# Batches 0 and 1 of a fused attention and feed-forward kernel: keys put into token order, v loaded in one DMA per block, weights issued at other places, four zero matmuls, attention steps placed by weight

## The chip, the cores and the metric

One core of a Trainium2 chip runs the whole program. The metric is the device time of one execution in microseconds (us). The engines are TensorE (PE; its weight loads are shown apart, as PEld), VectorE (DVE), ScalarE (ACT), GpSimd (POOL) and SyncE (SP). SP and POOL also issue DMAs.

## The reference, cut to what matters

Attention with a linear position bias (ALiBi) and a sliding window of 128 tokens, for 8 batches of 8 heads, 576 tokens and head size 64; then a feed-forward layer over all 8 x 576 = 4608 tokens. Inputs and output are fp32.

```python
scores = (q @ k.transpose(0, 1, 3, 2)) / 8.0
rel    = pos[:, None] - pos[None, :]
scores = where((rel >= 0) & (rel < 128), scores - slopes[h] * abs(rel), -1e9)
x      = softmax(scores) @ v                     # 8 batches, 8 heads
x      = x.transpose(0, 2, 1, 3).reshape(4608, 512)
h      = x @ w_in                                # 512 x 2048
out    = (h * sigmoid(beta * h)) @ w_out         # 2048 x 512
```

## The kernel before, in words

**Tokens, blocks, groups.** A batch has four full blocks of 128 tokens and a tail of 64. Attention works by batch and by pair of heads; the feed-forward layer works by groups of 512 tokens (g = 0 to 8), whose transposed input lies in the ring XT. The first half of the layer (`Hm`, L484) is, for each of 16 slices j of the 2048 features, four matmuls from W1 into a PSUM tile (hps, or hpx for some slices of group 0), a tanh on ACT (sig, L502) and the product on DVE (gT, L503). The second half (`OS`, L512) is 16 matmuls from gT and W2 for each 128 tokens, a copy on ACT (osb, L524) and a store. The weights arrive as four chunks each, issued by POOL (`load_w1` L268, `load_w2` L272); these DMAs cast from fp32 to bf16.

**Batches 0 and 1** have a path of their own. `get_pair` (L235) loads two heads of q or k, four neighbouring tokens to a partition; POOL casts to bf16 (`cast_pair`, L252); `TP` (L280) transposes both on PE into one PSUM tile and copies them to qkT, two copies on DVE. With c the place of a token in its group of four and r the number of the group, the copies put each block of 128 tokens in the order (c, r) instead of token order, for queries and keys alike. So v has to lie in the same order: `get` (L216) loads each full v block of these batches in four DMAs, one for each c (L222 to L228). `SP_` (L309) makes the scores of a pair of heads in two visits ("A" and "B"): matmuls that put the bias table into PSUM (SS), the query-key matmuls (L331), one exp on ACT to pt. `PVP` (L348) multiplies by v (L360) and normalizes on DVE (`norm`, L342: a reciprocal zs and a product xnp). `XP` (L367) transposes by a matmul with the permutation matrix perm, which puts queries back into token order, and DVE copies to XT (L372). The tails of both batches go through `TT`, `SCT`, `PV`, `X`. The constants for this path (ktok, qtok, rel, table, perm) come from `constants` (L109); qtok minus ktok is the distance of query and key in their permuted places. `constants_late` (L147) makes the table of the tails, relt and tablet.

**Batches 2 to 7** are loaded by block, cast on POOL, transposed by DMA (`DT`, L394). `SC` (L407) makes the scores of a pair; the exp (L430, four for a pair) takes its bias from the tile bias, one column for each head and half, and DVE multiplies by a mask (L434). `PV` (L445) and `X` (L465) follow.

**bias and the masks** are made in `constants_masks` (L189): POOL makes kpos by an iota (L193), 128x1, then the masks; sixteen small DVE instructions (L206) make bias from kpos.

**What sets the order.** PE, SP and POOL run in the order in which the program is written (L591). ACT and DVE have that too in the opening only (L592 to L645, batch 0 and the first slices of group 0); after it, a scheduler of the language chooses their order when the program is built. Every engine's queue is in order. After the opening, the program issues on SP the loads of batch 1 (the first waits for W1's second chunk, by `after(g, w1[1])`) and the tails of both batches; on POOL, in this order, the casts of batch 1 with W2's four chunks among them, then the casts of both tails, then `constants_masks`:

```python
        cast_pair(1, 2)
        w2 = [load_w2(0), load_w2(1)]
        cast_pair(1, 3)
        cast_v(1, 2)
        cast_v(1, 3)
        w2 += [load_w2(2), load_w2(3)]
        for b in range(2):
            cast_qk(b, 4)
            cast_v(b, 4)
        constants_masks()
```

On PE, the list `second` (L680) gives the steps of batch 1, two after each slice j of group 0's first half from j = 5 on. From group 1 on, `spread` (L717) places the attention steps of batches 2 to 7 (the list `att`: `SC`, `PV`, `X`, and the jobs that load, cast and transpose the next batch) between the matmul groups of the feed-forward layer: the same number of steps after each group.

**Buffers that matter here.** The loads share 13 tiles (fst). PE's transposes, PVP, XP, PV and X share two PSUM tiles (psum_t, tag "t"), hps has two, and all scores go through the one tile SS, except that visit "B" of batch 0 has a tile of its own, SX.

Of the kernel before, what the change touches and what calls it, by code (L numbers as in the profile page):

```python
# [15 lines left out]
P = 128  # L16
# [3 lines left out]
def kernel(  # L20
# [85 lines left out]

    def constants():  # L109
        nc.vector.memset(zeros[:], 0.0)  # L110
        nc.vector.memset(warm[:], 0.0)
        nc.scalar.activation(out=warm[:], in_=warm[:], func=ACTF.Exp)
        for _ in range(8):
            nc.tensor.matmul(
                SS[:, 0, :], lhsT=zeros[:, 0:P], rhs=zeros[:], start=True, stop=True,
                skip_group_check=True)
        for c in range(4):
            nc.gpsimd.iota(
                ktok[32 * c : 32 * c + 32], pattern=[[0, 1]], base=c, channel_multiplier=4,
                allow_small_or_imprecise_dtypes=True,  # L120
            )
        nc.gpsimd.iota(
            qtok[:].rearrange("p (c r) -> p c r", c=4), pattern=[[1, 4], [4, 32]], base=0, channel_multiplier=0,
            allow_small_or_imprecise_dtypes=True,
        )
        make_identity(nc, ident[:])
        nc.gpsimd.iota(
            nat[:], pattern=[[1, P]], base=0, channel_multiplier=0,
            allow_small_or_imprecise_dtypes=True,
        )  # L130
        nc.vector.tensor_scalar(
            out=qtok[:], in0=qtok[:], scalar1=ktok[:, 0:1], scalar2=None, op0=ALU.subtract)
        for a, cmp in ((0, ALU.is_lt), (1, ALU.is_ge)):
            nc.vector.tensor_scalar(
                out=pen[:], in0=qtok[:], scalar1=0.0, scalar2=FAR, op0=cmp, op1=ALU.mult)
            nc.vector.scalar_tensor_tensor(
                out=rel[:, a], in0=qtok[:], scalar=float(P * a), in1=pen[:], op0=ALU.add,
                op1=ALU.add)
        nc.vector.tensor_copy(out=rel[:, 2], in_=rel[:, 0])
        for h in range(H):  # L140
            nc.vector.tensor_scalar_mul(table[:, h], rel[:], -slopes[h] / qscale)
        for i in range(2):
            nc.vector.memset(VS[i][:, :, :, D : D + 1], 1.0)
        nc.vector.tensor_scalar(
            out=perm[:], in0=nat[:], scalar1=ktok[:, 0:1], scalar2=None, op0=ALU.is_equal)

    def constants_late():  # L147
        nc.gpsimd.iota(
            relt[:, 0], pattern=[[1, 64]], base=0, channel_multiplier=-1,
            allow_small_or_imprecise_dtypes=True,  # L150
        )
        nc.gpsimd.affine_select(
            out=relt[:, 0], in_=relt[:, 0], pattern=[[1, 64]], base=0, channel_multiplier=-1,
            compare_op=ALU.is_ge, fill=FAR,
        )
        for c in range(4):
            rows = slice(32 * c, 32 * c + 32)
            nc.gpsimd.iota(
                relt[rows, 1], pattern=[[1, 64]], base=P - c, channel_multiplier=-4,
                allow_small_or_imprecise_dtypes=True,  # L160
            )
            nc.gpsimd.affine_select(
                out=relt[rows, 1], in_=relt[rows, 1], pattern=[[-1, 64]], base=c - 1,
                channel_multiplier=4, compare_op=ALU.is_ge, fill=FAR,
            )
# [47 lines left out]
    fs = {}  # L213
    staged = {}

    def get(what, b, sb, eng=None):  # L216

        rows = ROWS[sb]
        src = {"q": q, "k": k, "v": v}[what]
        f = fst_pool.tile([P, H, D], F32, name="fst", tag="fst")  # L220
        fs[what, b, sb] = f
        if what == "v" and b < 2 and sb < 4:  # L222
            for c in range(4):
                (eng or nc.sync).dma_start(
                    out=f[32 * c : 32 * c + 32],
                    in_=src[b, :, P * sb : P * sb + P, :].rearrange(
                        "h (r c) d -> c r h d", c=4)[c],
                )  # L228
            return
        return nc.sync.dma_start(  # L230
            out=f[0:rows],
            in_=src[b, :, P * sb : P * sb + rows, :].rearrange("h p d -> p h d"),
        )
# [18 lines left out]
    def cast_pair(b, p):  # L252
        t = bst_pool.tile([P, 2, 4, 2 * D], BF16, name="bst", tag="bst")
        staged[b, "p", p] = t
        for i, w in enumerate("qk"):
            nc.gpsimd.tensor_copy(
                out=t[:, i].rearrange("r c (h d) -> r h c d", d=D),
                in_=fs.pop((w, b, "p", p))[:].rearrange("r h (c d) -> r h c d", d=D))
# [21 lines left out]
    def TP(b, p):  # L280
        src = staged.pop((b, "p", p))
        tps = psum_t.tile([P, 2, 4, P], BF16, name="tps", tag="t")
        for i in range(2):
            for c in range(4):
                nc.tensor.transpose(out=tps[:, i, c], in_=src[:, i, c], identity=ident[:])
        qk = QK[b % 2]
        for i in range(2):
            nc.vector.tensor_copy(
                out=qk[:, i, p, 0:FULL].rearrange("d (n c r) -> d c n r", n=4, c=4),
                in_=tps[:, i].rearrange("d c (n r) -> d c n r", n=4))  # L290

    def TT(b):

# [252 lines left out]
    def pvx(b, qbs):  # L546
        r = []
        for qb in qbs:
            r += [(None, lambda g=g, qb=qb: PV(b, qb, g)) for g in range(2)]
            if qb != qbs[0]:  # L550
                r.append(((b, qb - 1), lambda qb=qb: X(b, qb - 1)))
        r.append(((b, qbs[-1]), lambda: X(b, qbs[-1])))
        return r

    def merged(a, c):
# [11 lines left out]
    for b in range(2, B):  # L567
        here = []
        for m in range(2):
            a = [(None, lambda b=b, m=m, p=p: SC(b, m, p)) for p in range(NP)]  # L570
            here += merged(a, before)
            before = pvx(b, ((0, 1), (2, 3, 4))[m])
        if b + 1 < B:
            js, all_, n = jobs(b + 1), here, len(here)
            here = []
            for i, step in enumerate(all_):
                while js and js[0][0] * n <= 23 * i:
                    here.append((None, js.pop(0)[1]))
                here.append(step)
            here += [(None, j) for _, j in js]  # L580
        att += here
    att += before
    place = {key: n + 1 for n, (key, _) in enumerate(att) if key}

    def place_of(tok):
        b, s = divmod(tok - 1, S)
# [4 lines left out]
    with tc.manual_schedule(engines={ENG.PE, ENG.SP, ENG.Pool}):  # L591
        with tc.manual_schedule(engines={ENG.Activation, ENG.DVE}):  # L592
            for w in ("p0", "p1", "v0", "v1", "p2", "p3", "v2", "v3"):
                n = int(w[1])
                if w[0] == "p":
                    get_pair("q", 0, n)
                    get_pair("k", 0, n)
# [30 lines left out]
            PVP(0, "B", 0)  # L628
            PVP(0, "B", 1)
            XP(0, 0)  # L630
            PVP(0, "B", 2)
            XP(0, 1)
            PVP(0, "A", 3)
            XP(0, 2)
            PVP(0, "B", 3)
            betas()
            constants_late()
            opening.close()
# [13 lines left out]
        g = get_pair("q", 1, 0)  # L652
        after(g, w1[1])
        get_pair("k", 1, 0)
        for n in range(1, NP):
            get_pair("q", 1, n)
            get_pair("k", 1, n)
            if n == 1:
                get("v", 1, 0)
                get("v", 1, 1)  # L660
# [68 lines left out]

        def wrap(it, n):  # L730
# [55 lines left out]
```

## Time and profile before

| | |
|---|---|
| median of 3 runs | 364.48 us (363.73 to 366.2) |
| the profiled execution | 362.3 us |
| its span in the trace | 360.4 us |
| mean granted PE clock | 0.981 |
| data read and written | 36.71 MB and 9.44 MB |
| DMA packets under 512 B | 125840 of 136511 |

The profile shows one execution. Its span runs from the first to the last instruction; the time of an execution is a little longer. Busy time is given in us and as a share of the span for each engine; the clock is a share of full speed and is given by slice of the span. The DMA share is the mean busy time of the core's 16 DMA engines as the records tell it; in this trace it passes 1 in places. In the lists of instructions, `out<-in` names the tiles, `L` the line in the kernel, and the words in brackets say how long the engine had waited before and for what. The page's lines on where the chain of work that ended last spent its time:

```profile
PE 70%; DMA 11%; DVE 8%; ACT 5%; issue 3%; SPq 2%; POOL 1%; POOLq 0%; ACTq 0%
PE ops L518 32%; PE hps L495 28%; DMA fst<-in_k_dram 5%; PE SS L420 4%; ACT pt L430 3%; DMA fst<-in_v_dram 3%; DVE pt L434 3%; DVE gT L503 3%; PE pv L459 2%; PE pv L455 2%; PE xt L470 2%; DMA W<-in_moe_w_in_dram 2%; ACT sig L502 1%; DMA fst<-in_q_dram 1%; SPq L240 1%
```

The first line adds up the chain by engine, the second by engine, tile and line. Six tenths of the chain are the matmuls of the feed-forward layer.

### The profile page before, as it was taken

The numbers are of one execution on the slowest core, as the hardware profiler recorded it, in microseconds if no ns is written. First come the engines' busy times: TensorE is split into PE (matmuls) and PEld (weight loads), VectorE is DVE, ScalarE is ACT, GpSimd is POOL, SyncE is SP. The second block draws the span as 40 slices with busy tenths as digits, with TensorE's granted clock in tenths as the row PEclk, the third lists the DMA queues.
The fourth block names the chain that finished last, engine by engine and source line by source line (L and its number), as shares of the span: only waits on it lengthen the run. The fifth ranks groups of instructions, "written<-read, shape, count | busy, mean of one in ns | idle before, by whom it ended". The sixth has DMA issues, their size and how long they took to land.

```text
span 360.4 us, 6325 instructions
## 1 busy us (share of the span) xinstructions
PE 327.8 (91%) x2323; PEld 155.4 (43%) x2365; DVE 202.6 (56%) x448; ACT 206.4 (57%) x392; POOL 109.6 (30%) x214
## 2 busy tenths in 40 slices
PE   6777847798799999989999999999999999999995
PEld 2343413343345444444444444444444444544442
DVE  6456528554565578456738764875487546615500
ACT  2615623456756679457746776676677755525511
POOL 5597445403543442333132414131200010010010
PEclk9989969999899999999999999999999999999999
DMA  6799899995999999992928792962100010020012
GB/s 172 181 198 249 172 185 206 207 159 125 200 201 244 249 188 222 210 218 62 214 88 178 163 218 93 189 156 65 60 0 32 31 58 29 3 84 4 31 58 87
DMA packets 136511, 49.45 MB, mean 137 GB/s; under 512 B 125840, under 2 KB 134048, under 8 KB 136480
## 3 DMA queue, kind: packets, MB, share of 16 engines
q1 hardware_dynamic: 129536, 35.94, 51.4%
q0 software_dynamic: 6944, 13.11, 14.3%
q8 instruction: 18, 0.29, 0.4%
q14 instruction: 13, 0.11, 0.1%
HBM read 36.71 MB, written 9.44 MB: 128 GB/s over the span
## 4 chain that ended last, share of the span: by engine, by line
PE 70%; DMA 11%; DVE 8%; ACT 5%; issue 3%; SPq 2%; POOL 1%; POOLq 0%; ACTq 0%
PE ops L518 32%; PE hps L495 28%; DMA fst<-in_k_dram 5%; PE SS L420 4%; ACT pt L430 3%; DMA fst<-in_v_dram 3%; DVE pt L434 3%; DVE gT L503 3%; PE pv L459 2%; PE pv L455 2%; PE xt L470 2%; DMA W<-in_moe_w_in_dram 2%; ACT sig L502 1%; DMA fst<-in_q_dram 1%; SPq L240 1%
## 5 line engine op out<-in xcount | busy, mean ns | idle before, releaser
L495 PE MATMUL hps<-XT,W 128*128 128x512 bf16 x543 | 141.9, 385 | 5.4 <-DVE gT L503 2.6
L502 ACT ACTIVATE sig<-hps,beta_h 128x512 bf16<-128x512 f32 x140 | 96.0, 691 | 79.4 <-PE hps L495 73.9
L518 PE MATMUL ops<-W,gT 128*128 128x512 bf16 x552 | 137.9, 380 | 1.6 <-issue 0.5
L503 DVE SCALAR_TENSOR_TENSOR gT<-sig,hps 128x512 bf16<-128x512 bf16 x140 | 94.9, 683 | 62.8 <-ACT sig L502 62.2
L430 ACT ACTIVATE pt<-SS,bias 128x256 bf16<-128x256 f32 (+1 forms) x192 | 75.0, 477 | 13.0 <-PE SS L420 13.0
L495 PEld LDWEIGHTS <-W 128*128 128x128 bf16 x576 | 52.2, 98 | 61.6 <-issue 11.9
L518 PEld LDWEIGHTS <-gT 128*128 128x128 bf16 x576 | 52.3, 98 | 57.1 <-issue 1.9
L531 POOL DMA_DIRECT2D out_dram<-osb x34 | 18.4, 542 | 188.7 <-ACT osb L524 188.7
L434 DVE TENSOR_TENSOR pt<-pt,mask 128x1024 bf16<-128x1024 bf16 x48 | 38.1, 795 | 16.4 <-ACT pt L430 16.1
L524 ACT ACTIVATE osb<-ops 128x512 f32<-128x512 f32 x36 | 21.7, 603 | 41.3 <-PE ops L518 40.9
L262 POOL CAST vs<-fst 128x512 bf16<-128x512 f32 (+1 forms) x40 | 24.1, 613 | 25.8 <-DMA fst<-in_v_dram 24.4
L344 DVE RECIPROCAL zs<-pv 128x4 f32<-128x4 f32 (+1 forms) x80 | 13.7, 175 | 28.6 <-PE pv L459 19.2
L345 DVE TENSOR_TENSOR xn<-pv,zs 128x256 bf16<-128x256 f32 (+1 forms) x64 | 26.8, 421 | 1.6
L249 POOL CAST bst<-fst 128x512 bf16<-128x512 f32 (+1 forms) x32 | 20.2, 630 | 11.2 <-DMA fst<-in_q_dram 8.7
L420 PE MATMUL SS<-qkT 64*128 64x256 bf16 (+2 forms) x240 | 19.2, 254 | 2.8 <-ACT pt L430 2.8
L459 PE MATMUL pv<-vs,pt 128*128 128x65 bf16 x240 | 20.6, 193 | 0.5 <-DVE pt L434 0.5
L476 DVE COPY XT<-xt 128x512 bf16<-128x512 bf16 (+1 forms) x32 | 12.3, 384 | 15.3 <-PE xt L470 15.0
L250 POOL CAST bst<-fst 128x512 bf16<-128x512 f32 (+1 forms) x32 | 19.6, 613 | 3.7 <-DMA fst<-in_k_dram 3.3
L459 PEld LDWEIGHTS <-pt 128*128 128x128 bf16 x240 | 16.0, 97 | 7.1 <-DVE pt L434 0.6
L337 ACT ACTIVATE pt<-SS 128x768 bf16<-128x768 f32 (+1 forms) x12 | 10.6, 881 | 14.5 <-PE SS L331 14.5
L420 PEld LDWEIGHTS <-qkT 64*128 64x128 bf16 x240 | 8.2, 94 | 22.4 <-issue 22.0
L455 PE MATMUL pv<-vs,pt 128*128 128x65 bf16 x192 | 17.4, 193 | 0.1
(77 smaller groups left out, 172.2 us busy)
## 6 DMA issues: line engine op xcount, KB each, us to landing
out_dram<-osb POOLq DMA_DIRECT2D x34, 256.0 KB, 2.5
fst<-in_q_dram SPq DMA_DIRECT2D x32, 256.0 KB, 4.8
fst<-in_k_dram SPq DMA_DIRECT2D x32, 256.0 KB, 4.9
fst<-in_v_dram SPq DMA_DIRECT2D x24, 256.0 KB, 3.9
fst<-in_v_dram SPq DMA_DIRECT2D x32, 64.0 KB, 4.1
W<-in_moe_w_in_dram POOLq DMA_DIRECT2D x4, 512.0 KB, 6.7
W<-in_moe_w_out_dram POOLq DMA_DIRECT2D x4, 512.0 KB, 9.1
fst<-in_q_dram SPq DMA_DIRECT2D x8, 128.0 KB, 3.7
```

What stands on the lines that cost most here:

```text
L262: return nc.gpsimd.tensor_copy(out=VS[b % 2][0:rows, sb, :, 0:D], in_=fs.pop(("v", b, sb))[0:rows])
L345: nc.vector.tensor_tensor(out=xn, in0=pv[0:nq, :, 0:D], in1=zs[0:nq].broadcast_to([nq, 4, D]), op=ALU.mult)
L420: nc.tensor.matmul(o, lhsT=qk[64 * e : 64 * e + 64, 1, p, P * kb : P * kb + P], rhs=qk[64 * e : 64 * e + 64, 0, p, P * kb : P * kb + nq], ...
L430: nc.scalar.activation(out=pt[:, e, cols], in_=sps[:, e, cols], func=ACTF.Exp, scale=qscale, bias=bias[:, half, h : h + 1],)
L434: nc.vector.tensor_tensor(out=pt[:], in0=pt[:], in1=masks[m][:], op=ALU.mult)
L455: nc.tensor.matmul(pv[:, hl, 0 : D + 1], lhsT=weights(b, qb - 1, h, 1), rhs=vs[:, qb - 1, h, 0 : D + 1], start=True, stop=False,)
L459: nc.tensor.matmul(pv[:, hl, 0 : D + 1], lhsT=weights(b, qb, h, 0), rhs=vs[:, qb, h, 0 : D + 1], start=qb == 0, stop=True,)
L495: nc.tensor.matmul(hps[:], lhsT=W1[:, c, bass.ts(j, P)], rhs=XT[:, c, c0 : c0 + TOKG], start=(c == 0), stop=(c == NDM - 1),)
L502: nc.scalar.activation(out=sig[:], in_=hps[:], func=ACTF.Tanh, scale=beta_h[:, j : j + 1])
L503: nc.vector.scalar_tensor_tensor(out=gts[g][:, j, :], in0=sig[:], scalar=1.0, in1=hps[:], op0=ALU.add, op1=ALU.mult)
L518: nc.tensor.matmul(ops_, lhsT=gT[:, j, i * P : i * P + P], rhs=W2[:, j, :], start=(j == 0), stop=(j == NFF - 1),)
L524: nc.scalar.mul(osb[:], ops_, 0.5)
```

## The change

- **Keys in token order.** In `TP` the copy of k moves from DVE to ACT and writes the keys in token order (a strided output); the copy of q stays on DVE and keeps the order (c, r). k is loaded, cast and transposed before q.
- **v in one DMA.** With keys in token order, `get` loads every v block of batches 0 and 1 like all others, in one DMA instead of four.
- **Constants.** qtok becomes the distance by itself (an iota that also counts down over partitions), so a DVE subtraction goes; the second half of relt takes one iota and one select instead of four of each.
- **XT copies of batch 0** go from DVE to ACT.
- **Zero matmuls.** `idle(1)`, one 512-column matmul of zeros into SS, stands on PE ahead of `XP(0, 0)`, `XP(0, 1)` and `XP(0, 2)` and behind `PVP(0, "B", 3)`.
- **Weights.** W1's first chunk is issued before `cast_pair(0, 3)` and its second right behind it; the second was behind `cast_v(0, 3)`. W2's last two chunks are issued before `cast_v(1, 2)` and `cast_v(1, 3)` instead of behind them.
- **Steps by weight.** A step of `att` has a weight: 3 for `SC`, 2 for `PV` and `X`, 0 for a job; `spread` gives each matmul group the same weight of steps, not the same number.

```diff
+    def idle(n):
+        for _ in range(n):
+            nc.tensor.matmul(
+                SS[:, 0, :], lhsT=zeros[:, 0:P], rhs=zeros[:], start=True, stop=True,
+                skip_group_check=True)
...
         nc.gpsimd.iota(
-            qtok[:].rearrange("p (c r) -> p c r", c=4), pattern=[[1, 4], [4, 32]], base=0, channel_multiplier=0,
-            allow_small_or_imprecise_dtypes=True,
+            qtok[:].rearrange("p (c r) -> p c r", c=4), pattern=[[1, 4], [4, 32]], base=0,
+            channel_multiplier=-1, allow_small_or_imprecise_dtypes=True,
         )
...
-        nc.vector.tensor_scalar(
-            out=qtok[:], in0=qtok[:], scalar1=ktok[:, 0:1], scalar2=None, op0=ALU.subtract)
...
-        if what == "v" and b < 2 and sb < 4:
-            for c in range(4):
-                (eng or nc.sync).dma_start(
-                    out=f[32 * c : 32 * c + 32],
-                    in_=src[b, :, P * sb : P * sb + P, :].rearrange(
-                        "h (r c) d -> c r h d", c=4)[c],
-                )
-            return
...
-        for i, w in enumerate("qk"):
+        for i, w in ((1, "k"), (0, "q")):
             nc.gpsimd.tensor_copy(
...
-        for i in range(2):
+        for i in (1, 0):
             for c in range(4):
                 nc.tensor.transpose(out=tps[:, i, c], in_=src[:, i, c], identity=ident[:])
         qk = QK[b % 2]
-        for i in range(2):
-            nc.vector.tensor_copy(
-                out=qk[:, i, p, 0:FULL].rearrange("d (n c r) -> d c n r", n=4, c=4),
-                in_=tps[:, i].rearrange("d c (n r) -> d c n r", n=4))
+        nc.scalar.copy(
+            out=qk[:, 1, p, 0:FULL].rearrange("d (r c) -> d c r", c=4), in_=tps[:, 1])
+        nc.vector.tensor_copy(
+            out=qk[:, 0, p, 0:FULL].rearrange("d (n c r) -> d c n r", n=4, c=4),
+            in_=tps[:, 0].rearrange("d c (n r) -> d c n r", n=4))
...
-        nc.vector.tensor_copy(
+        (nc.vector.tensor_copy if b else nc.scalar.copy)(
             out=XT[:, p, b * S : b * S + FULL], in_=xt[:].rearrange("d n q -> d (n q)"))
...
+            w1.append(load_w1(0))
             cast_pair(0, 3)
-            w1.append(load_w1(0))
+            w1.append(load_w1(1))
             TP(0, 3)
...
             cast_v(0, 2)
             cast_v(0, 3)
-            w1 += [load_w1(n) for n in range(1, 4)]
+            w1 += [load_w1(n) for n in range(2, 4)]
             PVP(0, "B", 0)
             PVP(0, "B", 1)
+            idle(1)
             XP(0, 0)
...
         cast_pair(1, 3)
+        w2 += [load_w2(2), load_w2(3)]
         cast_v(1, 2)
         cast_v(1, 3)
-        w2 += [load_w2(2), load_w2(3)]
...
-            start = done
+            total, at = sum(w for _, _, w in att[done:target]), 0
             for n, it in enumerate(items):
                 it()
                 if waiting:
                     store()
-                to = start + (target - start) * max(0, n + 1 - first) // (last - first)
-                while done < min(target, to):
+                to = total * max(0, n + 1 - first) / (last - first)
+                while done < target and at + att[done][2] / 2 <= to:
                     att[done][1]()
+                    at += att[done][2]
                     done += 1
```

`constants_masks` and its place in the program are not touched by the diff.

More of the change, by code (lines that the diff above doesn't have):

```diff
@@ L112, in constants @@
         nc.scalar.activation(out=warm[:], in_=warm[:], func=ACTF.Exp)
[L113 to L116, printed above, removed]
+        idle(8)
         for c in range(4):
@@ L155, in constants_late @@
         )
-        for c in range(4):
[L157 to L160, printed above, removed]
-            )
[L162 to L165, printed above, removed]
+        nc.gpsimd.iota(
+            relt[:, 1], pattern=[[1, 64]], base=P, channel_multiplier=-1,
+            allow_small_or_imprecise_dtypes=True,
+        )
+        nc.gpsimd.affine_select(
+            out=relt[:, 1], in_=relt[:, 1], pattern=[[-1, 64]], base=-1,
+            channel_multiplier=1, compare_op=ALU.is_ge, fill=FAR,
+        )
         for h in range(H):
@@ L214, with get @@
     staged = {}
-    def get(what, b, sb, eng=None):
+    def get(what, b, sb):
         rows = ROWS[sb]
@@ L221, in get @@
         fs[what, b, sb] = f
-        if what == "v" and b < 2 and sb < 4:
-            for c in range(4):
-                (eng or nc.sync).dma_start(
-                    out=f[32 * c : 32 * c + 32],
-                    in_=src[b, :, P * sb : P * sb + P, :].rearrange(
-                        "h (r c) d -> c r h d", c=4)[c],
-                )
-            return
         return nc.sync.dma_start(
@@ L548, in pvx @@
         for qb in qbs:
-            r += [(None, lambda g=g, qb=qb: PV(b, qb, g)) for g in range(2)]
+            r += [(None, lambda g=g, qb=qb: PV(b, qb, g), 2) for g in range(2)]
             if qb != qbs[0]:
-                r.append(((b, qb - 1), lambda qb=qb: X(b, qb - 1)))
-        r.append(((b, qbs[-1]), lambda: X(b, qbs[-1])))
+                r.append(((b, qb - 1), lambda qb=qb: X(b, qb - 1), 2))
+        r.append(((b, qbs[-1]), lambda: X(b, qbs[-1]), 2))
         return r
@@ L569 @@
         for m in range(2):
-            a = [(None, lambda b=b, m=m, p=p: SC(b, m, p)) for p in range(NP)]
+            a = [(None, lambda b=b, m=m, p=p: SC(b, m, p), 3) for p in range(NP)]
             here += merged(a, before)
@@ L577 @@
                 while js and js[0][0] * n <= 23 * i:
-                    here.append((None, js.pop(0)[1]))
+                    here.append((None, js.pop(0)[1], 0))
                 here.append(step)
-            here += [(None, j) for _, j in js]
+            here += [(None, j, 0) for _, j in js]
         att += here
     att += before
-    place = {key: n + 1 for n, (key, _) in enumerate(att) if key}
+    place = {key: n + 1 for n, (key, _, _) in enumerate(att) if key}
     def place_of(tok):
@@ L595 @@
                 if w[0] == "p":
+                    get_pair("k", 0, n)
                     get_pair("q", 0, n)
-                    get_pair("k", 0, n)
                 else:
@@ L626 @@
             cast_v(0, 3)
-            w1 += [load_w1(n) for n in range(1, 4)]
+            w1 += [load_w1(n) for n in range(2, 4)]
             PVP(0, "B", 0)
             PVP(0, "B", 1)
+            idle(1)
             XP(0, 0)
             PVP(0, "B", 2)
+            idle(1)
             XP(0, 1)
             PVP(0, "A", 3)
+            idle(1)
             XP(0, 2)
             PVP(0, "B", 3)
+            idle(1)
             betas()
@@ L650, in tail @@
                     lambda: X(b, 4)]
-        g = get_pair("q", 1, 0)
+        g = get_pair("k", 1, 0)
         after(g, w1[1])
-        get_pair("k", 1, 0)
+        get_pair("q", 1, 0)
         for n in range(1, NP):
+            get_pair("k", 1, n)
             get_pair("q", 1, n)
-            get_pair("k", 1, n)
             if n == 1:
```

## Prediction

> **What bounds the kernel now.** I read the engine shares first, then the chain of waits in order of time, then the timeline where the chain leaves the PE, the busy time by stretch, and the DMA records.
>
> ```profile
> PE 327.8 (91%) x2323; PEld 155.4 (43%) x2365; DVE 202.6 (56%) x448; ACT 206.4 (57%) x392; POOL 109.6 (30%) x214
> PEclk9989969999899999999999999999999999999999
> ```
>
> The PE is busy 91% of the span and from 100 us on has hardly a gap; its 33 us of idle time lie in the first 100 us and at the very end. This change works on the first 100 us. The chain there:
>
> ```profile
> 41.09 8.25 DMA fst<-in_v_dram
> ...
> 50.06 0.32 PE pv L360 x3
> ...
> 59.36 0.97 DVE bias L206 x16
> ```
>
> A v load of batch 1 holds the PE until 50.06, and at 59.36 sixteen small DVE instructions (bias, made from kpos) are on the path. The timeline at those places:
>
> ```profile
> 41.64 0.34 PE L360 MATMUL pv<-vs,pt 128*128 128x65 bf16 x6
> ...
> 42.37 0.34 PE L331 MATMUL SS<-qkT 64*128 64x256 bf16 x4
> ...
> 50.06 0.32 PE L360 MATMUL pv<-vs,pt 128*128 128x65 bf16 x3 [4.92 <-POOL vs L262]
> ...
> 58.24 0.61 POOL L262 CAST vs<-fst 64x512 bf16<-64x512 f32 x1 [3.73 <-DMA fst<-in_v_dram]
> ...
> 58.81 0.14 POOL L193 IOTA kpos<- 128x1 f32 x1
> ...
> 59.27 1.05 DVE L206 TENSOR_SCALAR bias<-kpos 128x1 f32<-128x1 f32 x16
> ```
>
> Read the last three together: POOL makes kpos only after the cast of batch 1's last v block, and that cast waited 3.73 us for its load. So kpos at 58.81 is a time of the DMA stream, not of POOL. Busy time by stretch (PE, PEld, DVE, ACT, POOL, granted clock, DMA share, GB/s):
>
> ```profile
> 15.50:18.00 2.50, 1.92 (x22) 0.84 (x20) 0.99 (x4) 1.55 (x2) 1.97 (x4) 1.00 0.48 38
> 18.00:36.00 18.00, 14.00 (x119) 7.24 (x119) 10.67 (x26) 6.57 (x10) 14.73 (x35) 0.91 1.15 223
> 36.00:38.00 2.00, 0.88 (x12) 0.30 (x6) 0.85 (x2) 1.02 (x1) 0.00 (x0) 1.00 0.43 107
> ...
> 41.00:42.50 1.50, 1.50 (x16) 0.75 (x14) 1.16 (x5) 1.50 (x2) 1.50 (x4) 1.00 0.62 93
> ...
> 50.00:54.00 4.00, 3.72 (x22) 1.68 (x22) 1.61 (x5) 1.48 (x2) 3.84 (x8) 0.50 1.17 154
> ...
> 88.00:92.00 4.00, 1.65 (x13) 0.78 (x13) 1.98 (x3) 3.52 (x10) 0.00 (x0) 0.97 1.26 229
> 92.00:95.00 3.00, 2.67 (x10) 0.78 (x10) 0.88 (x2) 2.17 (x6) 1.45 (x3) 0.50 1.35 222
> ```
>
> The DMA engines are full (share about 1.15) from 10 to 62 us but for three holes. After each PE pause the clock is 0.50 for some microseconds. Records between 46 and 48 us, where v loads and the W2 loads are both under way (number, MB, share):
>
> ```profile
> q0 software_dynamic: 311, 0.32, 92.8%
> q1 hardware_dynamic: 312, 0.08, 29.6%
> ```
>
> The two queues alternate one record for one record, whatever the record's size: a 1024-byte weight record goes with every 256-byte record of v.
>
> **The step that decides.** Outside the opening DVE's order is the scheduler's, and the built order of the changed kernel moves bias. DVE's queue there, in order (changed kernel's lines):
>
> ```
> gT  <- sig,hps        (j = 6)
> qkT <- tps            (q of batch 1, pair 1)
> bias <- kpos   x16    waits for POOL
> zs, xnp <- pv         (PVP(1,"A",0))
> gT  <- sig,hpx        (j = 7)
> qkT <- tps            (q of batch 1, pair 2)
> ```
>
> Before, bias stands 25 instructions later, behind the norm of the second-last PVP of batch 1, where DVE arrives at 59.27, just after kpos. POOL's order is written out by hand and still has kpos behind all casts of batch 1 and of both tails. DVE runs its queue in order (the trace of before shows it in the built order), so from about 36 us, where it finishes the q copy of pair 1 (36.43 + 0.42 before), it now waits for kpos. Queued behind the wait: the norm of PVP(1,"A",0). PE goes on until PVP(1,"A",1), whose PSUM slot that norm must free (41.64 before).
>
> When is kpos? Before: 58.81. Holes that the one-DMA v loads and the earlier W1 can fill, at a full share of 1.15: 2.50 x (1 - 0.48/1.15) = 1.5, 2.00 x (1 - 0.43/1.15) = 1.3, 1.50 x (1 - 0.62/1.15) = 0.7, together -3.4. Against this, all of W2 is now issued before batch 1's last two v casts and so alternates ahead of the tail loads; before, 230 weight records ran between 58 and 61 us, after the v load: 230 x 0.096 us / 16 engines = +1.4. Between W1's second chunk and its last two, which wait for the cast of v, a new hole of 0 to 1.4 us, estimated from chunk 0 (5.5 us from issue to landing, 512 x 0.1 / 16 = 3.2 of it records): +0.7. So kpos at 58.81 - 3.4 + 1.4 + 0.7 = 57.5; bounds 55.4 (holes filled, nothing given back) and 60.9 (no hole filled, both costs).
>
> Then 0.15 of iota, 1.05 of bias, 0.6 of zs and xnp (0.17 + 0.42): PVP(1,"A",1) at 59.3. gT 0.69 and the q copy 0.42 more: the scores of SP_(1,"A",2) at 60.55 instead of 42.37: **+18.2**.
>
> The Trainium skill ("DMA: Bandwidth & Descriptors", Rules for kernel authors) advises to issue a DMA early and wait late, since the fixed setup then overlaps; by that rule the earlier W2 costs nothing and the sum is 1.4 lower. The row above disagrees: beside W2 that v load took 8.25 us, the ones just before it 2.7 to 3.3.
>
> **The other parts.**
> - The stall of 4.92 at 50.06 goes: PVP(1,"B",0) comes at about 63, long after its v (49.34 before, at most a few us later). **-4.9.** Late next is nothing of DMA: both tails and W2 have landed too.
> - bias leaves its old place, where 0.97 of it was on the path before the XT copy at 60.24: **-1.0**.
> - Clock: PE idles some 20 us and restarts at 0.50. Before, the same happened at 50.06 and cost 3.72/2 = 1.9 until 54. Taken as the same, **0**; bounds 0 and +1.9 (twice that). The Trainium skill ("TensorE: Matmul & The Clock Gate", Part 1) has free-running windows of 3.4 us, so 3.4 to 6.8 us cold; by it the loss is 1.7 to 3.4 and the sum -0.2 to +1.5.
> - Steps by weight: between 88 and 95 PE loses 2.35 idle and 2.67/2 = 1.3 at half clock, because score steps of batch 2 stand close and ACT paces them. In the new order no two stand without a matmul group (0.86) between, but ACT's work is the same: **-1.5**; bounds -4 (all gone) and +1.5 (later steps crowded instead).
> - All else lies under DVE's wait, 17 us of cover, and counts 0. If the cover were gone: four zero matmuls 4 x 0.22 to 0.42, at most 1.7; eight k copies on ACT, each priced between 0.60 (osb, 597 ns for 512 columns) and 0.81 (exp, 768 columns), nearest 0.60, and as built the q copy (0.42) waits for the k copy, so a pair takes 1.1 instead of 0.76: up to +2.5; XT copies 0.69 on DVE to 0.60 on ACT, -0.4; SP 32 v issues of 0.45 become 8 of 0.6, -9.6 of SP, off the path; six constants fewer on POOL, -1.2, one on DVE, -0.29; W1's second chunk ahead of the v casts on POOL: v of batch 0 (17.63) 2 earlier to 2 later. None outlasts 57 us.
> - Transposes of batch 2 follow kpos on POOL, no later than before, and PE wants them 11 us later: 0.
>
> Sum: 18.2 - 4.9 - 1.0 - 1.5 = +10.8. The profiled execution took 362.3 (span 360.4 and 1.9 around it): 373.1. The runs' median is 1.006 of it (364.48/362.3): **375**.
>
> **Rivals.**
> 1. kpos comes early and the kernel gets faster. Scores at kpos + 3.05, so the change is kpos + 3.05 - 42.37 - 4.9 - 1.0 - 1.5 = kpos - 46.7: it breaks even at 46.7. Earlier, down to no wait, it gains 4.9 + 1.0 + 1.5 and the clock's 1.9: 353 x 1.006 = 355. For it: one DMA per v block frees SP. Against: the tails land behind W1 and W2 whatever SP does, and the holes are 3.4, not 12. Chance 0.06; near break-even (365) 0.03.
> 2. W1 beside batch 0's v, the k-then-q copies and the new hole push the loads further, or the weighted order crowds ACT: all upper bounds, 373.1 + 3.4 + 1.9 + 3.0 = 381.4, in runs 384; beyond that 0.07.
> 3. The weighted steps bring the whole 4 and the holes are all filled: 373.1 - 2.1 - 2.5 = 368.5, in runs 371. Inside the forecast's range.
>
> **Numbers.** Forecast 0.84, rival 1 0.06, break-even 0.03, beyond 384 0.07. The range runs from rival 3 to rival 2: 370 to 384, about 0.82. Within 1% is about what a measurement can tell from none: faster 0.06, same 0.03, slower 0.91.
>
> **What would show it.** DVE idle before bias by some 20 us, ended by POOL kpos, and a PE gap to about 59 ended by DVE xnp; kpos between 55 and 61; no wait for vs at PVP(1,"B",0); clock 0.50 after the restart; fewer waits on ACT in batch 2's first scores. Wrong if kpos comes before 47, or DVE isn't held.

## The result, and the profile after

| | before | changed |
|---|---|---|
| median (range, runs) | 365.0 us (363.73 to 366.2, 4) | 374.25 us (373.62 to 375.9, 4) |
| profiled execution, its span | 362.3, 360.4 | 375.9, 374.0 |
| mean granted PE clock of the profiled execution | 0.981 | 0.967 |

The ratio is 1.0261, 95% interval 1.0211 to 1.0311. The profiled execution of the changed kernel is the longest of its four and that of the kernel before is shorter than its other runs, so the two traces lie 13.6 us apart where the medians lie 9.3 apart; what is read from the traces below adds up to 13.6. Of the executions below, one of e1 (364.84 us) and one of e12 (362.11 us, the profiled one) fell in a slower state of the chip and are left out of the ratios and of e12's median.

The changed kernel's page, engine shares and clock by slice:

```profile
PE 332.9 (89%) x2369; PEld 157.0 (42%) x2369; DVE 200.1 (54%) x435; ACT 217.1 (58%) x404; POOL 110.2 (29%) x208
...
PEclk9889966989999999999999999999999999999999
```

PE's idle time grew from 33 to 41 us and its busy time by 5.1 us. Four zero matmuls at the 0.42 us of the prediction's upper price are at most 1.7 of these; the clock is at 0.6 in the sixth and seventh slice (47 to 65 us). Some matmul records are missing in both traces (hps has 543 of 576 before, 560 now), so the busy times compare only roughly. The chain of waits in order of time at that place (start, length, what):

```profile
36.92 15.97 DMA fst<-in_q_dram
...
53.04 0.61 POOL bst L240
53.65 0.56 POOL bst L241
54.20 0.56 POOL vs L253
54.76 0.10 POOL kpos L192
...
54.89 1.06 DVE bias L205 x16
...
56.08 0.44 DVE xnp L337
...
56.56 0.51 PE pv L352 x6
```

Before, the DMA piece here was the load of v(1,3). Now it is the q load of the second tail, then POOL's three casts of that tail, kpos, bias, and only then the norm that PE waits for. The timelines of POOL, DVE and PE there (in brackets: idle before, and what ended it):

```profile
53.04 0.61 POOL L240 CAST bst<-fst 64x512 bf16<-64x512 f32 x1 [0.69 <-DMA fst<-in_q_dram]
...
54.72 0.13 POOL L192 IOTA kpos<- 128x1 f32 x1
```

```profile
39.71 0.42 DVE L280 COPY qkT<-tps 128x512 bf16<-128x512 bf16 x1 [0.50 <-ACT qkT L278]
54.89 1.06 DVE L205 TENSOR_SCALAR bias<-kpos 128x1 f32<-128x1 f32 x16 [14.76 <-POOL kpos L192]
55.87 0.17 DVE L336 RECIPROCAL zs<-pv 128x4 f32<-128x4 f32 x1
56.08 0.42 DVE L337 TENSOR_TENSOR xnp<-pv,zs 128x256 bf16<-128x256 f32 x1
```

```profile
43.62 1.04 PE L487 MATMUL hps<-XT,W 128*128 128x512 bf16 x4
56.56 0.51 PE L352 MATMUL pv<-vs,pt 128*128 128x65 bf16 x6 [11.90 <-DVE xnp L337]
56.88 0.83 PE L312 MATMUL SS<-table,ident 128*128 128x384 bf16 x2
57.64 0.50 PE L323 MATMUL SS<-qkT 64*128 64x256 bf16 x4
```

DVE stands still for 14.76 us with the first bias instruction at the head of its queue; PE runs on as far as `PVP(1, "A", 1)`, then idles 11.9 us. Busy time by stretch (PE, PEld, DVE, ACT, POOL, clock, DMA share, GB/s):

```profile
15.50:18.00 2.50, 1.57 (x23) 0.92 (x24) 1.03 (x3) 1.37 (x3) 2.28 (x8) 1.00 1.21 181
36.00:38.00 2.00, 1.55 (x16) 1.00 (x17) 0.40 (x1) 1.01 (x2) 2.00 (x4) 1.00 1.23 205
41.00:42.50 1.50, 1.50 (x19) 0.87 (x19) 0.00 (x0) 0.97 (x2) 0.00 (x0) 1.00 1.20 198
...
56.50:62.50 6.00, 5.94 (x39) 2.79 (x40) 3.02 (x8) 3.06 (x4) 4.40 (x14) 0.50 0.82 156
79.90:83.90 4.00, 4.00 (x19) 1.50 (x18) 1.71 (x3) 1.38 (x2) 0.00 (x0) 0.59 0.02 4
```

The three holes in the DMA stream are full. After the pause PE works six microseconds at half clock, and once more at 80 us.

Where the two traces part and meet is seen by the start of the same gT instruction (group, slice) in each. Times in us; the other columns are differences to the kernel before. The experiments are told below. The execution of the kernel before that was traced (362.3 us) is 1.4 to 3.7 us below the medians of that kernel (363.7 to 366.0), so gains look smaller here than between medians, and losses larger.

| gT | before | changed | e2 | e1 | e3 | e9 |
|---|---|---|---|---|---|---|
| 0, 0 | 29.17 | +2.22 | -1.52 | +2.58 | +2.38 | +3.49 |
| 0, 6 | 35.84 | +2.68 | +0.09 | +3.04 | +2.84 | +3.95 |
| 0, 8 | 42.58 | +15.31 | +0.21 | +3.50 | +3.29 | +4.40 |
| 0, 9 | 44.50 | +16.22 | +0.17 | +3.51 | +3.31 | +4.42 |
| 0, 10 | 52.85 | +11.55 | +12.27 | -2.21 | -2.42 | -1.31 |
| 0, 15 | 66.26 | +10.70 | +11.62 | -2.99 | -3.19 | -2.08 |
| 1, 1 | 71.21 | +11.96 | +11.61 | -1.47 | -3.19 | -0.63 |
| 2, 0 | 119.16 | +10.22 | +11.78 | -3.93 | -2.64 | -3.11 |
| 8, 14 | 341.48 | +13.60 | +11.42 | -0.99 | -2.74 | -3.48 |

For the changed kernel: +15.3 up to slice 8 (DVE's wait, the longer opening inside it), +0.9 in slice 9 (half clock), -4.7 at slice 10 (no stall for v), -0.85 by slice 15 (bias gone from its old place; every kernel with bias moved gains 0.6 to 1.0 there, but for e12 with 0.3), +1.3 (half clock at 80 us), -1.7 in batch 2's first scores, +3.4 from group 2 on.

### The profile page after: what moved, and what is told of

It is laid out like the page before. It is cut to its first block, busy times and chain, and to the rows that moved or that the text cites. A ratio compares the mean times of both kernels' runs of the same rounds, so it can differ in the third digit from the quotient of the medians.

```text
span 374.0 us, 6326 instructions
## 1 busy us (share of the span) xinstructions
PE 332.9 (89%) x2369; PEld 157.0 (42%) x2369; DVE 200.1 (54%) x435; ACT 217.1 (58%) x404; POOL 110.2 (29%) x208
## 4 chain that ended last, share of the span: by engine, by line
PE 67%; DVE 9%; DMA 8%; ACT 6%; POOL 4%; issue 2%; SPq 2%; POOLq 0%; ACTq 0%
PE ops L510 30%; PE hps L487 27%; DMA fst<-in_q_dram 8%; DVE pt L426 5%; ACT pt L422 4%; PE SS L412 3%; DVE gT L495 3%; PE pv L451 2%; ACT sig L494 2%; PE xt L462 1%; PE pv L447 1%; SPq L231 1%; POOL tablet L166 1%; POOL bst L247 1%; POOL W L260 1%
## 5 line engine op out<-in xcount | busy, mean ns | idle before, releaser
L510 PE MATMUL ops<-W,gT 128*128 128x512 bf16 x576 | 141.3, 379 | 0.0
L510 PEld LDWEIGHTS <-gT 128*128 128x128 bf16 x576 | 51.5, 98 | 54.5 <-issue 1.9
L426 DVE TENSOR_TENSOR pt<-pt,mask 128x1024 bf16<-128x1024 bf16 x48 | 41.8, 872 | 23.0 <-ACT pt L422 22.7
L253 POOL CAST vs<-fst 128x512 bf16<-128x512 f32 (+1 forms) x40 | 25.7, 651 | 21.0 <-DMA fst<-in_v_dram 20.8
L451 PE MATMUL pv<-vs,pt 128*128 128x65 bf16 x240 | 21.6, 193 | 0.4 <-DVE pt L426 0.4
L352 PE MATMUL pv<-vs,pt 128*128 128x65 bf16 x112 | 7.1, 213 | 13.0 <-DVE xnp L337 11.9
L447 PE MATMUL pv<-vs,pt 128*128 128x65 bf16 x192 | 17.9, 193 | 0.0
```

Of the source, the lines that this page charges most:

```text
L253: return nc.gpsimd.tensor_copy(out=VS[b % 2][0:rows, sb, :, 0:D], in_=fs.pop(("v", b, sb))[0:rows])
L426: nc.vector.tensor_tensor(out=pt[:], in0=pt[:], in1=masks[m][:], op=ALU.mult)
L447: nc.tensor.matmul(pv[:, hl, 0 : D + 1], lhsT=weights(b, qb - 1, h, 1), rhs=vs[:, qb - 1, h, 0 : D + 1], start=True, stop=False,)
L451: nc.tensor.matmul(pv[:, hl, 0 : D + 1], lhsT=weights(b, qb, h, 0), rhs=vs[:, qb, h, 0 : D + 1], start=qb == 0, stop=True,)
L510: nc.tensor.matmul(ops_, lhsT=gT[:, j, i * P : i * P + P], rhs=W2[:, j, :], start=(j == 0), stop=(j == NFF - 1),)
```

## The experiments

Theory: DVE's order puts bias, and with it the wait for kpos, ahead of batch 1's first norm, and this one place makes the kernel slower. Rival: the copies on ACT and the weights beside the loads make it slower, and the wait for bias only shows that.

### e1: the changed kernel, bias in the opening

```diff
-        nc.gpsimd.iota(kpos[:], ...)                 # constants_masks
-        for h in range(H): ... bias[:, half, h : h + 1] ...
+    def biases(): # the same iota and sixteen instructions
...
             betas()
             constants_late()
+            biases()
```

> The changed kernel, with the kpos iota put behind the tails' table on POOL (about 25 us) and the sixteen bias instructions in DVE's opening order, before the first gT, where DVE idles 3.84 us. Theory (DVE's wait for kpos is what costs): the wait of 14.8 us before bias and PE's 11.9 us at PVP(1,"A",1) go, and what is left of the change shows: opening +2.7 (the gT of slice 6 came 2.68 us later than before), v stall -4.9, old place of bias -1.0, half clock after the stall -1.9, batch 2's first scores -1.7, later steps by weight +3.4 (both read from where the two traces part and meet): -3.4, about 361 us, 357 to 363. Rival (the cost is in the copies on ACT and in W2 beside the loads, and bias only shows it): still above 368.

Measured: 361.43 us (ratio 0.9920 to the kernel before, 0.989 to 0.9951). DVE's line now, between beta_h and the first gT:

```profile
27.98 1.05 DVE L207 TENSOR_SCALAR bias<-kpos 128x1 f32<-128x1 f32 x16
31.76 0.69 DVE L497 SCALAR_TENSOR_TENSOR gT<-sig,hps 128x512 bf16<-128x512 bf16 x1 [2.73 <-ACT sig L496]
```

The same instructions at another place of two queues (kpos on POOL, bias on DVE) make 12.8 us between the medians, with the copies on ACT and the weights as in the changed kernel. The rival falls.

### e2: the kernel before, bias forced to the early place

```diff
         norm(xn[:, q0 : q0 + 2, :]..., pv, P, None)
+        if (b, vis, p) == (1, "A", 0):
+            after(late["zs"], late["bias"])   # the reciprocal waits for the last bias
```

> The kernel before, with one added dependence: the reciprocal of PVP(1,"A",0) waits for the last bias instruction, so that DVE has bias at the place where the changed kernel has it. Theory: scores of SP_(1,"A",2) at kpos + 3 = 58.8 + 3 = 61.9 instead of 42.4, +19.5, less the v stall 4.9 and bias's old place 1.0: +13.6, about 378 us (375 to 381). Rival (bias's place does not decide): 363 to 367.

Measured: 374.27 us (ratio 1.0277, 1.0217 to 1.0338), as slow as the changed kernel, with none of the seven parts of the change. What DVE and PE wait for between 36 and 66 us (total, times, longest):

```profile
DVE bias L206 <- POOL kpos L193: 12.5, 1, 12.5
```

```profile
PE tps L285 <- DVE xnp L345: 15.8, 1, 15.8
```

It is 3.7 less than expected: kpos came at 57.7, not 58.8, and PE was held one step later, at the transposes of `TP(1, 3)`.

### e7: the kernel before, bias in the opening

The diff of e1, on the kernel before.

> The kernel before, with kpos and bias in the opening as in the first run of this set. Theory: bias leaves the path at 59.3, at most -1.0: 363.5 to 365. If the kernel before had gained as much by this alone as the changed kernel does, the first run would say nothing of the change: that would be 361 or less.

Measured: 361.73 us (0.9926, 0.9888 to 0.9964), 2.6 less than the kernel before, where at most 1 was expected; its trace ends only 0.6 earlier. The traced execution of the kernel before was 2.0 faster than the median of this set and e7's was at its median, which is the other 2.0; why bias alone gains more than 1 us between the medians stays open. Here kpos stood behind the tails' table on POOL and held DVE until 30.5 us, which made the opening 4.4 us longer; the v stall took all of it back. With bias out of the way in both, the changed kernel (e1) and the kernel before differ by 0.3 us: all other parts of the change together bring nothing that can be measured. The remaining runs ask which parts gain and which lose.

### e3 and e9: steps by number, and by weight in the first spread only

Both on top of e1. e3 puts back the old `spread`; e9:

```diff
-        def spread(items, first, last, target):
+        def spread(items, first, last, target, even=False):   # even: every step weighs 1
...
-            spread(items, 0, len(items) - 3, target)          # groups 2 to 8
+            spread(items, 0, len(items) - 3, target, even=True)
```

> The first kernel of this set (changed kernel, bias in the opening) with attention steps spread by number again instead of by weight. Theory from the traces (weights gain 1.7 around 100 us and lose 3.4 between 167 and 270 us): 1.7 us faster than the first kernel, about 359. Rival (my step in the prediction, weights gain 1.5): 1.5 slower than the first kernel, about 362.5.

> The changed kernel with bias in the opening and weights in the first spread only. Theory: 3.4 faster than with weights everywhere (361.4), 2 faster than with numbers everywhere (359.9): about 358. Rival: as with numbers, 359.5 to 360.5. Against the run before it, it also has the dearer key copies (1.28 us against 0.42, eight of them): 1 to 2 slower than that one.

Measured: e3 359.9 (0.9898, 0.9863 to 0.9933), e9 358.26 (0.9863, 0.9808 to 0.9918), against 361.43 with weights everywhere. PE's waits from 110 to 280 us, e1 and then e3:

```profile
PE hps L489 <- DVE gT L497: 4.6, 5, 1.7
```

```profile
PE hps L489 <- DVE gT L497: 2.0, 5, 1.1
```

In the table above, the three traces with weights only up to group 1, or nowhere (e9, e3, e2), stay within 0.4 us of where they stood to the kernel before from group 2 on; the two with weights everywhere lose 2.9 and 3.4 there, nearly all in groups 4 and 5. The gain of weights lies in batch 2's first scores alone: 2.5 in e1 and e9, 1.7 in the changed kernel, between slice 1 of group 1 and group 2. Less waiting is the smaller part of it (from 84 to 110 us PE waits 3.3 us for ACT and DVE in the kernel before, 2.4 in e9). The larger is the clock: all five traces with steps by number (before, e2, e3, e7, e11) have a half-clock stretch of 3.4 us there, of the nine with weights only e12's, and that one gains just 0.9. Why the clock stays up is not shown.

From slice 1 of group 1 to the end, e1 loses 0.48 us to the kernel before and e3 0.45, so weights everywhere and numbers come out even in these traces; e3's lead of 1.7 is there before, 1.5 of it from half clock in e1 at 66 us. e9 gains 2.85 on the same stretch. The medians' intervals overlap between neighbours, so the sizes rest on the traces.

### e4: without the zero matmuls

```diff
-            idle(1)          # all four
```

> The changed kernel with bias in the opening, without the four zero matmuls. Theory (each stands in a wait for the ACT copy that frees XP's PSUM slot, and the clock is 1.0 there anyway): no change, 361.4 within 0.7. Rivals: they keep the clock up (a window of half clock in 24 to 31 us, up to 1.7 slower without them), or they are on the path (three of 0.36 us, 1.1 faster without them).

Measured: 361.73 (0.9958, 0.9923 to 0.9993): no difference to e1 that the intervals tell. The waits that they fill are waits of 0.2 to 0.5 us for DVE's norm, not for the ACT copy as I had it. In the trace without them the first gT is 0.8 later, with half clock from 27 to 30 us instead of 21 to 24; one trace of each can't say that this belongs to the zero matmuls.

### e5: the copy of k on DVE

```diff
-        nc.scalar.copy(
+        nc.vector.tensor_copy(
             out=qk[:, 1, p, 0:FULL].rearrange("d (r c) -> d c r", c=4), in_=tps[:, 1])
```

> The changed kernel with bias in the opening, and the token-order copy of k on DVE instead of ACT, ahead of q's. In the opening the ACT copy took 1.28 to 1.30 us, and the q copy waits for it. Theory (ACT is slow at this strided output, DVE is not: its q copy takes 0.42): 8 x 0.86 less between transposes and scores, of which the opening's four are on the path: first gT 2.5 to 3.4 earlier, batch 1's partly: 358 to 359.5. Rival (the stride is as dear on DVE): about 361.5, with DVE copies of 1.2 us.

Measured: 359.79 (0.9877, 0.9796 to 0.9959). The copies, minimum/median/maximum in ns, in e1 on ACT (k, and an XT copy of as many columns) and in e5 on DVE (k, then q):

```profile
L280 ACT COPY qkT<-tps x8: 1284/1294/1307, 5.6 to 47.9; 128x512 bf16<-128x512 bf16 x8
```

```profile
L366 ACT CAST XT<-xtp x4: 585/585/585, 24.6 to 30.0; 128x512 bf16<-128x512 f32 x4
```

```profile
L280 DVE COPY qkT<-tps x8: 1280/1292/1304, 6.8 to 46.7; 128x512 bf16<-128x512 bf16 x8
L282 DVE COPY qkT<-tps x8: 402/441/449, 7.9 to 48.5; 128x512 bf16<-128x512 bf16 x8
```

The theory falls on the price: writing every fourth column costs 1.29 us on either engine, three times the copy with runs of 32 columns. The median is 1.6 less than e1's all the same, though the intervals overlap; the trace shows 0.5 of that in the opening and 0.8 in batch 1, and it lacks e1's half-clock stretch at 66 us.

### e6: the changed kernel, W2 as before

```diff
-        w2 += [load_w2(2), load_w2(3)]
         cast_v(1, 2)
         cast_v(1, 3)
+        w2 += [load_w2(2), load_w2(3)]
```

> The changed kernel as it is (bias behind kpos in batch 1), with W2's last two chunks behind the casts of v(1,2) and v(1,3) as before. My step in the prediction: the earlier W2 alternates with the tail loads and costs kpos 1.4 us, so kpos 53.3 instead of 54.7 and the whole 1.4 us less, about 372.9. Rival (those casts come early now, at about 38 us, so the place makes hardly a difference): kpos within 0.5 of 54.7, time as the changed kernel's 374.3.

Measured: 375.88 (1.0317, 1.0222 to 1.0413); kpos at 55.04, against 54.72. No gain. v(1,2) and v(1,3) land at 36.8 and 38.2 here, so the old place of W2's last chunks is 38.8 us instead of 36.1: too little to matter.

### e10, e11, e13: what took the v stall away

e10 is e1 with each v block in four DMAs of 32 neighbouring rows. e11 is the kernel before with W1 and W2 issued as in the changed kernel and bias in the opening (kpos ahead of the tails' table). e13 is e9 with W1 and W2 issued as before.

```diff
+        if what == "v" and b < 2 and sb < 4:                       # e10
+            for c in range(4):
+                nc.sync.dma_start(
+                    out=f[32 * c : 32 * c + 32],
+                    in_=src[b, :, P * sb + 32 * c : P * sb + 32 * c + 32, :].rearrange(
+                        "h p d -> p h d"))
+            return
```

> The changed kernel with bias in the opening, and each full v block of batches 0 and 1 loaded by four DMAs of 32 rows again (token order kept). It asks what took the v stall away. Theory (the 24 further issues of SP do: they pushed v(1,3) behind W2's issue, where the records alternate): v(1,3) lands near 49 again instead of 37 to 38, PE waits for vs at PVP(1,"B",0) by some 4 us, 365 to 367. Rival (W1 two chunks earlier did it): no wait for vs, 361 to 362.5.

> The kernel before (keys, v in four DMAs, XT copies, steps by number all as before) with W1 and W2 issued as in the changed kernel, kpos ahead of the tails' table and bias behind beta_h in the opening, where DVE idles 3.61 us. Theory (W1's second chunk, issued earlier, starts batch 1's loads earlier, and that alone takes the v stall away): v(1,3) lands near 40, no wait for vs at PVP(1,"B",0), the opening is not longer, so slices 10 on come some 5 to 6 us sooner than before: 357 to 360. Rival (token-order keys or the one-DMA v are needed too): a wait for vs of 2 us or more, 361 to 362.5.

> The last run but one (changed kernel, bias in the opening, weights in the first spread only: 358.3) with W1 and W2 issued in the order of the kernel before. It closes the square on the v stall: four strided DMAs with the old and the new order of the weights both kept it, four DMAs in token order with the new order lost it, one DMA with the new order lost it; here one DMA with the old order. Theory (SP has at most eight DMAs under way, so v in one DMA is issued before W2 whatever W1 does): v(1,3) is issued before W2's first chunk and lands by 42, no wait for vs, 357.5 to 359.5. Rival (the earlier W1 is needed as well): v(1,3) lands near 49, PE waits for vs by 3 us or more, 361 to 363.

Measured: e10 360.16 (0.9891, 0.9814 to 0.9968), e11 360.72 (0.9927, 0.9887 to 0.9967), e13 357.7 (0.9784, 0.9722 to 0.9845). From the DMA records, in us:

| | v of batch 1 | weights' order | last part of v(1,3): issued, landed | W2's first issue | cast of v(1,3) done | PE at PVP(1,"B",0) | stall for v there |
|---|---|---|---|---|---|---|---|
| before | 4, strided | old | 41.09, 49.34 | 39.57 | 50.01 | 44.82 | 4.9 |
| e11 | 4, strided | new | 42.06, 50.43 | 38.80 | 51.10 | 48.26 | 2.6 |
| e10 | 4, in rows | new | 38.97, 47.20 | 37.53 | 47.87 | 47.89 | none |
| e13 | 1 | old | 33.19, 38.56 | 35.69 | 39.55 | 49.25 | none |
| e9 | 1 | new | 31.17, 36.85 | 33.55 | 38.90 | 49.30 | none |

e11's wait, as the list of PE's waits from 36 to 60 us has it, and e10's cast and matmuls:

```profile
PE pv L362 <- POOL vs L264: 2.6, 1, 2.6
```

```profile
47.25 0.62 POOL L262 CAST vs<-fst 128x512 bf16<-128x512 f32 x1 [4.91 <-DMA fst<-in_v_dram]
...
47.89 0.42 PE L361 MATMUL pv<-vs,pt 128*128 128x65 bf16 x8
```

The one-DMA v alone is enough, as expected for e13 (e13 and e9 end within 0.02 us of each other in their traces); the earlier W1 alone is not (e11). Four DMAs in neighbouring rows with the earlier W1 (e10) show no stall either, but not because v comes early: its last part takes 8.2 us, as e10's theory has it, and its cast ends at 47.87, just when PE gets there. PE comes 3.1 us later than in the kernel before; had it come as early, it would have waited an estimated 3 us (47.87 less 44.82). e10's time lies below the ranges of both its theory and its rival.

What the rows share is the place of v(1,3)'s last part against W2's first issue: in the three kernels with four DMAs it is issued 1.4 to 3.3 us behind and takes 8.2 to 8.4 us to land, in the two with one DMA the whole block is issued ahead and takes 5.4 and 5.7. That the order makes the difference is read from these five rows; no run changes it alone. e11 also shows what the earlier W1 does where v comes in four: PE waited 3.6 us for v of batch 0 in the opening, and the last part of that v, issued at 13.81 with W1's records under way beside it, took until 20.89 to land (15.11 and 17.63 in the kernel before). So the later stall was only partly a loss.

### e12: e11 with weights in the first spread

e11 and the weights in the first spread only (the diff of e9).

> The run before this one with steps by weight in the first spread (group 1) only, by number from group 2 on. Theory (weights gain about 2.5 us at batch 2's first scores, and lose 3.4 to 3.9 between 161 and 270 us by crowding gT's, seen in every trace with weights and in none without): 2 to 2.5 faster than the run before it. Rival (the gain at batch 2 is only the place where a half-clock window falls): no difference beyond 0.7.

Measured: 357.7 (0.9836, 0.9763 to 0.9909), 3.0 less than e11. The gain rests on the times alone: the trace, of the execution at 362.11, ends 0.2 us before e11's and gains 0.9 at batch 2's first scores, with half clock from 97 to 100 us, so the rival about the half-clock window is not ruled out. e12, e9 and e13, at 357.7 to 358.3 us, all beat both kernels; e9 is 0.6 slower than e12, where 1 to 2 were expected for its dearer key copies, and that is within the spread of the executions.

## Why the prediction was right

The time (375 forecast, 374.25 measured), the direction and the mechanism are right: e1 and e2 show the mechanism from both sides. The terms of the sum, against the trace of the changed kernel:

- **The step that decides, +18.2: measured +15.3.** The step that was off is the time of kpos, forecast at 57.5 within 55.4 and 60.9, measured 54.72, below both bounds. The three holes are full (DMA share 1.20 to 1.23), for which the sum has -3.4 of the -4.1. The other 0.7 may lie in two stretches that were not counted as holes: 13 to 15.5 us went from a share of 1.03 to 1.27 and 38 to 41 us from 0.88 to 1.10, while 18 to 36 us fell from 1.15 to 1.13; by the same rule that is an estimated 0.8 us. The two terms against it, +1.4 for W2 ahead of the tail loads and +0.7 for a hole in W1, weren't there: from 11 to 18 us the share is never below 1.09, so W1 left no hole; e6 takes the W2 term away and kpos does not come earlier (55.04), because the casts ahead of which W2 was put wait for loads that now land at 36 to 37 us. So the prediction's other reading, that the earlier W2 costs nothing, was the right one. The rest, kpos + 3.05 to the scores, measured 2.9 (54.72 to 57.64); the parts that the prediction lists add up to 2.91, not 3.05. It is another path of the same length: the q copy ends at 57.43, and PE comes to the scores without a pause, behind its own matmuls at half clock.
- **The v stall, -4.9: -4.7. The old place of bias, -1.0: -0.85.** Right. That nothing of DMA is late next holds too.
- **The clock, 0 with +1.9 as a bound: +0.9 after the pause, and +1.3 more at 80 us.** PE lost about 3.0 us at half clock after the pause (5.94 us busy at 0.50), against 1.9 before; this lies in the 1.7 to 3.4 that the prediction gives beside its own bounds. The second stretch had no place in the sum.
- **Steps by weight, -1.5 with +1.5 as a bound: -1.7 at batch 2's first scores, most of it by a half-clock stretch that stayed away, then +3.4.** The net +1.7 lies just past the bound. The step took one stretch for the whole: I read 88 to 95 us, where steps stand close, and priced "later steps crowded instead" without a row for it. e1 against e3 and e9 shows the loss, nearly all in groups 4 and 5, where PE waits for gT.
- **All else under cover, 0.** Right as long as the wait covers it: the opening came 2.2 us later, and nothing of that is left behind the wait. Without the cover (e1) it is there, and a mis-sized price is the likely reason: the k copy was priced at 0.60 to 0.81 us by rows of contiguous copies and took 1.29, and PE's waits for qkT from 3 to 32 us grew from 3.0 to 6.9 us. No run takes the strided copy away, so this is argued. The zero matmuls cost nothing either way (e4).

So the terms missed by -2.9 (kpos) and by +2.2 (clock) and +3.2 (weights), with 0.2 and 0.15 at the stall and bias: +2.85, which is the 375.9 of the profiled execution against the 373.1 of the sum, within rounding. The number came out well partly since these offset each other. Rival 1's price, 355 with no wait, was wrong by 6: e1 shows 361.4, with the opening's 2.6 to 3.5 and the weights' later loss still in it. The warning sign that PE runs to about 59 us was right in kind (56.56, ended by DVE xnp), kpos "between 55 and 61" missed by 0.3. DVE's wait was 14.76 us and not "some 20": it began at 40.1 and not at about 36, behind the longer opening and the k copies, and kpos came 2.8 earlier than forecast.

## What to carry to other kernels

Where a scheduler sets an engine's order, compare the built order before and after a change, and ask of every instruction that moved forward what it waits for: here one wait at the head of a queue was worth more than everything else the change did. Small set-up work that feeds a late stage should have its producer early, in a stretch where both engines idle, so that no order can turn it into a block (in e7 kpos was early in the program but late on POOL, and held DVE in the opening). And a stage whose end is set by a stall hides gains and losses ahead of it, so price each part once under the cover and once without it.

## What the runs showed of the hardware that was not expected

- **A strided write is dear on both engines.** The copy of 128 x 512 bf16 from PSUM with an output step of four columns (8 bytes) takes 1.29 us on ACT and on DVE; on DVE, with runs of 32 columns, 0.40 to 0.45; on ACT, contiguous and from fp32, 0.585. The Trainium skill ("SBUF — State Buffer", the note on cachelines under Door 1) lets bf16 step up to 8 elements without loss, two hits in a 16-byte line being enough; these rows disagree for writes.
- **SP never has more than eight of its DMAs under way in these traces.** In the kernel before, eight are issued between 24.12 and 27.78; the ninth at 30.36, the first having landed at 30.30; the next at 30.96, 31.70 and 33.15, where landings are at 30.94, 31.68 and 33.13. In e11 the last two parts of v(1,3) go at 40.85 and 42.06, behind landings at 40.84 and 42.04. A load in four parts so takes four of eight places, which moves the last part of v(1,3) behind W2's first issue (the table of e10 to e13). What sets the eight, the chip or the program, is not shown; with v in one DMA SP has seven at most.
- **Half-clock stretches of 3 to 4 us come or stay away with hardly a difference in the work.** e1 and e3 run the same PE instructions up to there, 0.2 us apart; the stretches 62.0 to 65.5 and 65.5 to 69.0 us in e1, then in e3:

```profile
62.00:65.50 3.50, 1.64 (x23) 0.88 (x22) 1.96 (x6) 1.25 (x2) 1.17 (x2) 0.98 1.02 211
65.50:69.00 3.50, 3.50 (x11) 1.08 (x11) 0.69 (x1) 0.69 (x1) 0.00 (x0) 0.53 1.17 209
```

```profile
62.00:65.50 3.50, 1.64 (x23) 0.95 (x22) 1.96 (x6) 1.04 (x2) 1.17 (x2) 1.00 1.11 201
65.50:69.00 3.50, 3.20 (x22) 1.48 (x21) 1.62 (x3) 1.50 (x3) 1.17 (x2) 1.00 0.92 194
```

With the same 1.64 us of work in the first stretch, e1 gets half clock in the second and loses 1.5 us, e3 doesn't. Differences of one or two microseconds between single traces of this kernel can be that. Nor does half clock follow each pause of PE, as the prediction says: in the trace of before the pauses of 4.92 and 1.66 us that end at 50.06 and 90.77 us are followed by it, those of 1.1 to 1.2 us that end at 33.7, 37.3 and 61.0 are not.
